# Transposes of the first part as pairs of 64-row halves, norms ahead as listed steps, and new written orders for the first part and the transition

## The chip, the cores and the metric

The kernel runs on one core of a Trainium2 chip. The metric is the device time of one execution in microseconds (us); the median of three runs before the change is 1122.0 us. The engines are TensorE (PE for matmuls, PEld for its weight loads), VectorE (DVE), ScalarE (ACT), GpSimd (POOL) and SyncE (SP), whose queue issues nearly all DMAs. Matmul results go to PSUM, eight banks of 512 float32 columns on 128 partitions.

## The reference

Two blocks follow each other. The first is attention with random features, for 8 batches, 8 heads, 576 rows and 64 columns a head, and 128 features; the second mixes by Fourier transforms and applies a two-layer perceptron, 512 wide and 2048 hidden.

```python
def phi(x):                                   # x is q or k, scaled; omega is 128 x 64
    h = np.einsum('bhsd,md->bhsm', x, omega) - np.sum(x * x, axis=-1, keepdims=True) / 2.0
    h = h - np.max(h, axis=-1, keepdims=True)
    return np.exp(h) / np.sqrt(m)
kv = np.einsum('bhsm,bhsd->bhmd', k_p, v)
z = np.sum(k_p, axis=2)
out = np.einsum('bhsm,bhmd->bhsd', q_p, kv) / (np.einsum('bhsm,bhm->bhs', q_p, z)[..., None] + 1e-06)
# the heads side by side: x is (8, 576, 512)
u = x + np.real(np.fft.fft(np.fft.fft(x, axis=1), axis=2))
un = (u - mean(u)) / np.sqrt(var(u) + 1e-06)
result = u + np.maximum(un @ w_ch1, 0.0) @ w_ch2
```

All is float32 in the kernel. The two weight matrices arrive as float64 and are narrowed on the chip.

## The kernel before

**First part.** A pair of heads is one unit of the attention, n = 0 to 31 (B * NP), three units in flight (`attn`, L668). `loads` brings k and q of a unit into one tile kq of 18 x 64 columns (L471, L474) on SP's queue. `transposed` (L590) turns the nine 128 x 128 pieces of kq on PE against the 128 x 128 identity `ident` (L607), in groups of 4, 4 and 1, each group into one bank; `evicted` (L611) copies a bank to the tile kqT, on ACT or DVE (L621, L623), and the bank is free. Matmuls with omega (L701) follow, for the first six units as 64-row halves of the array, later as 64 x 64 quarters. DVE takes the maxima (L644), ACT the exponentials e (L661). L735 makes kv in quarters. The nine pieces of e that belong to q are turned in the same way into qeT (groups of 1, 4, 4), but here the eviction also reorders rows, so that mirrored rows stand where the Fourier part wants them: each group is copied in two pieces, one of them read backwards. L782 and L790 multiply qeT with kv, two 64-column halves at a time; the quotient goes to x.

Once per batch `mix` (L823) folds x on DVE and POOL and multiplies with cosine and sine tables (L894, L904, L944, L955). `residual` (L980) joins the cosine part and the sine part: ACT copies one bank to bmp (L988), DVE makes difference and sum in three pieces each (L993 twice, L996), and both are added to x on DVE or POOL (L1005, L1006). The sum u goes to DRAM (`us`).

Beside it, `narrow` (L522) makes float32 weights out of the float64 ones in five elementwise steps, over ACT, POOL and DVE (L534 or L532, L537 to L544, L550). `plain_of` (L1205) runs the perceptron of the first four tiles of 128 tokens in the ordinary way (L1236, L1259): PE work that can stand wherever the attention leaves room. `norm_of` (L1130) normalises a tile and turns it with four 128 x 128 transposes (L1172, evicted at L1176). `warm` (L574) issues six matmuls on zeros at the start, `first` (L581) turns omega (L586).

**Second part.** Eight blocks of 512 tokens are multiplied by two levels of a seven-product scheme (L1727, L1878 and, for the second layer, L2178), from w1, its sums and sums stored in DRAM. The normalised tokens of later blocks reach it turned, through DRAM tiles `turned`. For blocks 1 to 3 (j) this is done by `ahead` (L1573): twelve tiles are loaded, normalised and turned in 32 x 32 pieces on DVE, nine of them in buffers that the attention leaves (kq, kqT), three in late ones. `wash` (L2288) marks three banks with matmuls on the identity before the second part (L2298).

**The order.** The kernel's Python code runs a listing: streams of `Step`s with an engine, buffers to take and give and banks ("bank" is one, "duo" two neighbouring ones). The next step is not chosen by cost; it is read from strings, `PICKS` (which waiting step is next, and for a step with a choice which engine) and `BANKS` for the first part, `PICKS2` and `BANKS2` for the second. So each engine's order is written out, and an instruction that waits holds all behind it on its engine. The pieces of `ahead` stand outside the listing: `BETWEEN` and `BETWEEN2` say after which number of placed steps a generator is advanced.

Of the kernel before, what the change touches and what calls it, by code (L numbers as in the profile page):

```python
# [41 lines left out]
class Clock(NamedTuple):  # L42
# [25 lines left out]
PICKS = (  # L68
    "40e0fff03eafdaege3OcdceefdcOdeccfgda37ghj0gjj7hlP79aj7ik97i8S7efhjffeHldffiehdjfdOihgihidaKedbhhciff"
    "ecgOfeejdfdPdeeedgifdffdefd8aiii88jhd8jP8b99i8e8jcddghjgheiifcOcdciieicgPgdefJcdghbkededfgcRbggb79ij"  # L70
    "8hi7hjafN9Haj9gfffeg8eif8hcej1jccc7ehidbhffLigebfbe6766gggfcbjahj9Ofghhjj8dQkkgT6jghff8de6dUjfhbgegh"
    "cefhafjUf8jgciSjOckkhjakkaeikggjlioklnhSgodoXON7l7l6nnj9icadc97cibf98ejH88a7edhMlhkmjjaQVijihkkfplSm"
    "okliljjilVaghVhnmljkmpjkhhnmkimlgglmbjpjjQ9d9alafhhdjlaMdjback0j766k7lh4g896ck6gkki77gij5ijhgj6dimni"
    "3ndjgi6Kc4jldlKikbkaijLhf75dcjlmklk36ci45jciekajkkkk5kihokeaeoLaioNlencidonbSiljjcmjjkboijTUUhgcfkik"
    "hiflkmeFF99nol5m8jT7naabda89Rbj97ecdl8cjilOgifkQb4acahg57ebbgabgdjkdTkk6eceebb5f9dg4R6ce486ggg6egfhh"
    "fg4g9egf5cbdhgPRhhcgjhggejigibLmHnbedijj6NOb7biihi9bgihMkaffPa8cijdhbdghbaeibNefffacjicigifi99975ih5"
    "jgj8699ajfg6g7fgefd65bO6Kalkkgd5jgjikagfldliPJpeoaeeefgdejadgilgScljiii5e65k56kl57k7j67S9lilk9gliih6"
    "ffkgec4fg4dbgg7fedaiP5gfbheefilddddddeghg9kbfncgghcfkkafkagGngb65p5Hopoj4bhoanbelli68bjjl5b7dlhighhi"
    "lflhpkgiWomjknmmmkimnjbjhn9jkmFKkfFgedccff6Wf7idUVhi8Th3fogbqp8fgmkeSdjna7ckenoghmnmffnjeo79q6547oa4"
    "nlkpd7aceonnc8blSVicilbhmjim8fh7SnnIl5mUkfjgfhhfhihg8ghfbS4kjf83j4lllb79jei8mnkblfnmmiolpilOUi9Mh5l5"  # L80
    "pmnaem79jjVmkbblek5iji9a9kffTgjikhiShfgjafhgfigh4g50PPP0ba5Pdh9dghdK77hgfdcbg8OO988jMehefibjjkellfcc"
    "PcdhQMihfQcffbKCf82b3c98cbcdcd6a299efgddbJaGQQbefLa9ecf74gg986HRgf9idg8kQeheff7be6ff2e5cc8fbcgdKP8f8"
    "9hN9Lc999bddcHcNb7Oc9effegd7ibhQeQ8haf7ccghhlUikhHW5lWmm5dkMQGM71fS6d1gdb99747ifddhIfdhhdhfdbihgiljn"
    "gWgijgg93ekKl8kEhIIbT3jjKgkb9k9eTfhkhlje34m49974iG66h68faHe6e7a79982975aI94a39c8cM8b4aa7ab984fge8eLM"
    "98b86ce8PbFPc9cbe6cKPf3a9b94fIdIQeJKbd876eJPdc5fNb7ffbf9JSS8RiLa4a7gPbajfgg8gdfhg2i2787Hf6OcdIN5d3LH"
    "accd46ddeKK72dJc7bbaa4bb9a9bc7c0777dghhdf7Bfddebd76ff1fddIe9949438686bc6aca85348dHcG7a5be957b55d1544"
    "9Gc1F5a9a68446344584584E59189970955888574443113301110"
)

BANKS = (  # L90
    "0102346120164024306243643016204164024320632462014021604606245062345042604670426420340267407231640260"
    "4524016460620240674206206415704602546064320143607264506402346234062732017426042106147026740260462462"
    "0410652604632452017205467402624060404256174302642060245016745202642016420634520520650162505605260250"
    "1675602501605204672016204567627450264102316742067460260462045642062637230724672402630145420640106240"
    "5264023026731602454230412046450416725730620424670121726154305610207453"
)

PLACES = "kkktttkktuuu"  # L100


BETWEEN = (
# [3 lines left out]
)  # L107


BETWEEN2 = (  # L110
    "006390119901259015590198902149023690236a0262a0265a0301a0329a0355a0426a0486b0528b0528b0550b0552b0563b"
    "0578b"
)
# [262 lines left out]
def kernel(  # L376
# [21 lines left out]
    KD = DM // 2 + 1  # L398
    QD = DM // 4
    KE = QD + 1  # L400
    K0 = DM // 8 + 1
    CV = 512
    P = 128

# [1990 lines left out]
```

## Time and profile before

| | us |
|---|---|
| median of three runs (1120.99 to 1122.96) | 1122.0 |
| profiled execution, first to last instruction (its span; no other time of it is given) | 1119.2 |
| first part, up to the first L1727 | 417.8 |
| second part | 701.4 |

In the profile, the first table gives the busy time of each engine. The windows give it stage by stage. In a group of instructions "L607 PE MATMUL banks<-ident,kq 128\*128 128x128" line 607 multiplies, with 128 rows and 128 columns of weights, a streamed operand (ident) into banks; 64\*128 are 64 rows and 128 columns. A float32 matmul that is no transpose appears as two passes, so as two records; a transpose is one. A record's own duration (some 275 ns for 128 columns) is longer than the distance between two of them, since they overlap; what one costs is read from a run of them on the chain or from two starts on the timeline.

### The profile page before, as it was taken

How to read it: one execution, taken by the hardware profiler on the slowest of the kernel's cores; microseconds unless marked ns; L12 is line 12 of the kernel's file. 1: busy time of each engine (PE TensorE's matmuls, PEld its weight loads, DVE VectorE, ACT ScalarE, POOL GpSimd, SP SyncE). 2: the span in 40 equal slices, each digit the busy share in tenths (PEclk: the TensorE clock that was granted, in tenths of full speed). 3: DMA queues.
4: the chain of work that ended last, by engine and by line, in shares of the span. 5: the costliest groups of instructions: out<-in, count | busy, mean ns of one | idle time of the engine just before them, and what ended most of it. 6: DMA issues, size and time to landing. Idle time of an engine off the chain costs nothing.

```text
span 1119.2 us, 31666 instructions
## 1 busy us (share of the span) xinstructions
PE 1108.4 (99%) x12467; PEld 1000.4 (89%) x12467; DVE 888.7 (79%) x1685; ACT 539.5 (48%) x1644; POOL 390.6 (35%) x401
## 2 busy tenths in 40 slices
PE   9999999999999999999999999999999999999998
PEld 7888888879868778999999889999889999889998
DVE  6999999987576767687697777888677888568895
ACT  7998898856536455623214452223463223331221
POOL 2443443553563348634413464000365000152000
PEclk9999999999999999999999999999999999999999
DMA  8856766665674669798896778747678656546453
GB/s 243 243 174 188 242 180 191 183 208 176 216 232 156 194 172 343 224 314 262 260 326 224 226 216 248 207 148 238 206 207 261 207 155 216 170 152 220 146 160 105
DMA packets 196549, 236.13 MB, mean 211 GB/s; under 512 B 53808, under 2 KB 120624, under 8 KB 196400
## 3 DMA queue, kind: packets, MB, share of 16 engines
q1 hardware_dynamic: 195904, 233.83, 68.1%
q8 instruction: 99, 1.62, 0.6%
q14 instruction: 50, 0.41, 0.1%
q10 hardware_dynamic: 496, 0.26, 0.1%
HBM read 182.13 MB, written 56.10 MB: 213 GB/s over the span
## 4 chain that ended last, share of the span: by engine, by line
PE 92%; DVE 3%; ACT 2%; DMA 2%; issue 0%; POOL 0%; SPq 0%; DVEq 0%; ACTq 0%
PE banks L2178 31%; PE banks L1727 27%; PE banks L1236 5%; PE banks L701 5%; PE banks L607 5%; PE banks L1259 5%; PE banks L1878 4%; PE banks L735 3%; PE banks L782 2%; PE banks L944 2%; PE banks L894 1%; ACT e L661 1%; DVE nmx L644 1%; PE banks L904 1%; DMA unw<-turned 1%; DMA raw<-in_moe_w_ch_dram 1%
## 5 line engine op out<-in xcount | busy, mean ns | idle before, releaser
L2178 PE MATMUL banks<-wl,sums 128*128 128x128 f32 x1792 | 219.8, 275 | 0.0
L2178 PEld LDWEIGHTS banks<-wl,sums 128*128 128x128 f32 x1792 | 210.6, 192 | 1.0 <-issue 0.3
L661 ACT ACTIVATE e<-banks,nmx 128x128 f32<-128x128 f32 x576 | 165.7, 441 | 23.3 <-DVE nmx L644 22.9
L644 DVE TENSOR_REDUCE nmx<-banks 128x8 f32<-128x1024 f32 (+1 forms) x96 | 89.3, 951 | 16.8 <-PE banks L701 12.4
L2178 PE MATMUL banks<-wl,hid 128*128 128x128 f32 x768 | 99.2, 275 | 0.3 <-DVE part L2154 0.3
L2178 PEld LDWEIGHTS banks<-wl,hid 128*128 128x128 f32 x768 | 92.8, 192 | 1.2 <-DVE part L2154 0.8
L2149 ACT ACTIVATE s<-banks 128x128 f32<-128x128 f32 x112 | 30.9, 277 | 113.6 <-PE banks L2178 103.5
L1727 PE MATMUL banks<-unw,wxw 128*128 128x256 f32 x352 | 85.4, 379 | 0.0
L701 PE MATMUL banks<-om,kqT 64*64 64x128 f32 (+1 forms) x2088 | 79.0, 275 | 1.7 <-ACT kv L751 1.3
L701 PEld LDWEIGHTS banks<-om,kqT 64*64 64x64 f32 (+1 forms) x2088 | 64.5, 138 | 12.7 <-issue 3.2
L2178 PE MATMUL banks<-wl,hx 128*128 128x128 f32 x576 | 74.2, 275 | 0.4 <-DVE part L2154 0.4
L1727 PEld LDWEIGHTS banks<-unw,wxw 128*128 128x128 f32 x352 | 66.6, 190 | 8.9
L1727 PE MATMUL banks<-rx,wxw 128*128 128x256 f32 x288 | 70.8, 379 | 0.0
L2178 PEld LDWEIGHTS banks<-wl,hx 128*128 128x128 f32 x576 | 69.4, 192 | 0.8 <-DVE part L2154 0.6
L1752 ACT ACTIVATE s<-banks 128x512 f32<-128x512 f32 x65 | 38.5, 596 | 65.1 <-PE banks L1727 60.0
L1727 PE MATMUL banks<-ttw,wxw 128*128 128x256 f32 x288 | 69.8, 379 | 0.0
L1236 PE MATMUL banks<-unT,w 128*128 128x128 f32 x512 | 65.4, 279 | 1.7 <-DVE qeT L621 1.7
L550 POOL TENSOR_TENSOR w<-w,raw 128x512 f32<-128x512 f32 x28 | 37.6, 1351 | 77.3 <-DVE raw L544 68.1
L2227 POOL TENSOR_TENSOR more<-more,part 128x512 f32<-128x512 f32 x2 | 2.6, 1315 | 176.6 <-ACT part L2220 176.6
L1236 PEld LDWEIGHTS banks<-unT,w 128*128 128x128 f32 x512 | 60.2, 192 | 4.5 <-issue 2.3
L1727 PEld LDWEIGHTS banks<-rx,wxw 128*128 128x128 f32 x288 | 54.5, 190 | 7.3
L1727 PEld LDWEIGHTS banks<-ttw,wxw 128*128 128x128 f32 x288 | 54.5, 190 | 7.3
(287 smaller groups left out, 2442.3 us busy)
## 6 DMA issues: line engine op xcount, KB each, us to landing
wl<-w2l SPq DMA_DIRECT2D x245, 256.0 KB, 3.9
wxw<-w1x SPq DMA_DIRECT2D x120, 256.0 KB, 3.1
raw<-in_moe_w_ch_dram SPq DMA_DIRECT2D x32, 512.0 KB, 4.8
kq<-in_k_dram SPq DMA_DIRECT2D x32, 288.0 KB, 4.5
kq<-in_q_dram SPq DMA_DIRECT2D x32, 288.0 KB, 4.5
vd<-in_v_dram SPq DMA_DIRECT2D x32, 288.0 KB, 5.4
ur<-us SPq DMA_DIRECT2D x30, 256.0 KB, 5.2
w2l<-sums SPq DMA_DIRECT2D x14, 512.0 KB, 4.9
```

The costliest lines, as they stand in the source:

```text
L550: eng.tensor_tensor(out=dst, in0=dst, in1=lof, op=ALU.add)
L607: nc.tensor.transpose(ps[:, (j - j0) * 128 : (j - j0 + 1) * 128], src(j), ident[:])
L644: nc.vector.tensor_reduce(nmx[:, :, 0:num], pps[:, :, 0 : MF * num].rearrange("p b (c m) -> p b c m", m=MF), axis=AX.X, op=ALU.max, negate ...
L661: nc.scalar.activation(out=e[:, c + (i if num == 1 else 0), :], in_=pps[:, i, MF * c : MF * c + MF], func=AF.Exp, bias=nmx[:, i, c : c + 1],)
L701: nc.tensor.matmul(pps[cols, c, MF * m : MF * m + MF], lhsT=kqT[rows, j, cols], rhs=om2[rows, :],)
L735: nc.tensor.matmul(kvp[cols, i, 0 : D + 1], lhsT=feature(r)[rows, cols], rhs=vds[n % NV][rows, r, :], start=(r == 0), stop=(r == R - 1),)
L1236: nc.tensor.matmul(hp[:, 0:TP], lhsT=w1[:, dc, 128 * fc : 128 * fc + 128], rhs=unTs[key][:, dc, :], start=(dc == 0), stop=(dc == NDC - 1),)
L1259: nc.tensor.matmul(yp[:, 0:DM], lhsT=hs[fc][:, 128 * i : 128 * i + 128], rhs=w2[:, fc, :], start=(fc == 0), stop=(fc == NFC - 1),)
L1727: nc.tensor.matmul(ps[:, span * f : span * f + span].rearrange("f (b q) -> f b q", q=Q), lhsT=left[:, P * f : P * f + P], rhs=right, start ...
L1752: nc.scalar.activation(out=s[:], in_=ps, func=AF.Copy)
L1878: nc.tensor.matmul(cell.rearrange("f t (b q) -> f t b q", q=Q), lhsT=w[:, d, col : col + 128], rhs=right[:, :, d].rearrange("f (t b) q -> ...
L2178: nc.tensor.matmul(ps[:, 0:128], lhsT=left[:, f], rhs=wls[head(j), i, n][:, f], start=start and f == 0, stop=(f == 3), skip_group_check=True,)
```

## The change

- **Halves.** Each 128 x 128 transpose becomes two instructions on 64 rows of the source and a 64 x 64 block of `ident`; the halves write to two neighbouring banks, r = 0 and 1 (`half_turned`). The groups are 4 and 5 for kqT and 5 and 4 for qeT, each in a "duo"; there is one copy per group. `ident` gets permuted blocks off its diagonal, so that the mirrored order of qeT is made by the transpose itself, which writes every fourth column of its bank (`spaced`); the second factor's columns are addressed accordingly in L782 and L790. Omega's and the norms' transposes are halved too.
- **Identity.** `ident` comes by DMA, first on SP's queue, instead of from POOL.
- **Mixing.** L944 writes even columns of the spectrum to every second column of the bank and odd ones between; the tables are ordered to suit. For two of the three row groups `residual` uses five ACT instructions, then two DVE additions of 257 columns instead of six pieces; the third group has the pieces as before.
- **Narrowing.** The third step may run on POOL, as two instructions.
- **Norms ahead** are ordinary steps of the listing: nine in the first part (buffers kq and turned), three in the second.
- **Orders.** All `PICKS` and `BANKS` strings are new.
- `NTURN` is 32, the number of units; what is for n >= NTURN never runs (a transpose of whole units on DVE, with loads in blocks).

```diff
+    eyes = np.zeros((2, D, 2, D), np.float32)
+    h_, s_, t_ = np.meshgrid(np.arange(2), np.arange(2), np.arange(16), indexing="ij")
+    turn_ = (32 * h_ + 2 * np.where(s_ == 1, 15 - t_, t_) + s_).ravel()
+    for r in range(2):
+        eyes[r, np.arange(D), r, np.arange(D)] = 1.0
+        eyes[r, turn_, 1 - r, np.arange(D)] = 1.0
+    nc.sync.dma_start(ident[:], nc.inline_tensor(eyes.reshape(128, 128), name="k_eyes").ap())
...
-    make_identity(nc, ident[:])
...
+    def half_turned(to, src, turn=False):
+        for r in range(2):
+            rows, cols = slice(D * r, D * r + D), slice(D * (r ^ turn), D * (r ^ turn) + D)
+            nc.tensor.transpose(to(r), src[rows], ident[rows, cols])
+
+    def spaced(ps, r, at, c):
+        out = ps[:, r, :]
+        return bass.AP(out.tensor, out.offset + at + c, [list(out.ap[0]), [128, 2], [67 - 2 * c, 2], [4, 16]])
...
             yield Step(
                 PE,
-                0.109 * m,
+                0.062 * m,
+                mode="rows",
                 after=after(j0, j1),
-                take=("bank",) + (("turned",) if j0 == 0 else ()),
+                take=("duo",) + (("turned",) if j0 == 0 else ()),
...
-                nc.tensor.transpose(ps[:, (j - j0) * 128 : (j - j0 + 1) * 128], src(j), ident[:])
-            yield Fork(evicted(dst, b, j0, j1, makes, order))
+                i = j - j0
+                def to(r):
+                    if not mirror:
+                        return ps[:, r, D * i : D * i + D]
+                    if j == 0:
+                        return ps[:, r, 0:D].rearrange("q (s t) -> q t s", s=2)
+                    c = (j - 1) % 4
+                    return spaced(ps, r, D * (j - c - j0), c)
+                half_turned(to, src(j), mirror and j > 0)
+            yield Fork(evicted(dst, b, j0, j1, makes, mirror))
...
-            ((0, 4), (4, 8), (8, R)),
+                ((0, 4), (4, R)),
...
-            ((0, 1), (1, 5), (5, R)),
+            ((0, 5), (5, R)),
...
-                    ab[p1 * n : p1 * n + np_, n, cols],
+                    ab[p1 * n : p1 * n + np_, n, m:KD:2],
...
-        yield Step(ACT, 0.28, take=("bmp",), give=(b1,))
...
+        if c < NL:
+            yield Step(ACT, 0.62, take=("bmp",), bias=0.1)
+            bmp, (aa, mi, pl) = taken()
+            nc.scalar.activation(out=mi[:, KD:], in_=pb[:, KD : KD + 1], func=AF.Copy)
+            nc.scalar.activation(out=pl[:, KD:], in_=pb[:, KD : KD + 1], func=AF.Copy, scale=-1.0)
+            nc.scalar.activation(out=aa[:, 1:KD:2], in_=pa[:, 1:KD:2], func=AF.Copy)
+            for k, mid in ((0, mi), (2, pl)):
+                nc.scalar.activation(out=aa[:, k:KD:4], in_=pa[:, k:KD:4], func=AF.Identity, bias=mid[:, KD:])
+            for last, (dst, op) in enumerate(((mi, ALU.subtract), (pl, ALU.add))):
+                yield Step(DVE, 0.34, give=(b0, b1) if last else (), bias=-0.1)
+                nc.vector.tensor_tensor(out=dst[:, 0:KD], in0=aa[:, 0:KD], in1=pb[:, 0:KD], op=op)
...
-        yield Step(DVE, 0.61, give=("sign",), port=True, bias=-0.99)
...
+        step = Step({DVE: 0.61, POOL: 3.0}, give=("sign",), port=True, bias=-0.99)
+        yield step
+        if step.eng == POOL:
+            nc.gpsimd.tensor_scalar(lof, lo, 2.0**-52, None, op0=ALU.mult)
+            nc.gpsimd.tensor_tensor(out=lof, in0=lof, in1=sign[:].bitcast(F32), op=ALU.mult)
...
-        yield Step(PE, 0.437, take=("bank",), give=("u",))
+        yield Step(PE, 0.26, mode="rows", take=("duo",), give=("u",))
...
+            half_turned(lambda r: tp[:, r, D * dc : D * dc + D], u[:, 128 * dc : 128 * dc + 128])
...
-        yield Step(NONE, give=(b,))
+        yield Step(NONE, after=("held",), give=(b,))
```

More of the change, by code (lines that the diff above doesn't have):

```diff
@@ L411 @@
     NWIDE = 6
+    NTURN = 32
     TP = 128
@@ L726, in attn @@
             mode="quarters",
-            after=tuple(("e", n, t) for t in range(3)) + (("vd", n),),
+            after=tuple(("e", n, t) for t in ((0, 1, 2) if n < NTURN else (0, 2, 3))) + (("vd", n),),
             take=("duo",),
@@ L1065 @@
     unTs = {}
-    Q = 32
     turned = {}
@@ L2359 @@
     listing.run(
-        [wash(), late_turns(), late_norms(), halves(), load_leaves(), token_sums(0), w1_sums(), w1_inner(), w1_stored()],
+        [wash(), late_turns(), late_norms(), halves(), load_leaves(), token_sums(0), w1_sums(), w1_inner(), w1_stored()]
+        + [ahead(3, i, "ur", late) for i in range(1, TB // 128)],
         picked(PICKS2, 3),
         BANKS2,
-        betweens(BETWEEN2),
     )
```

456 lines of the change are left out of this document (282 added, 174 removed).

## The prediction

> **What bounds the kernel now.** First the page's busy shares and its chain of waits, which ask for the engine that sets the end; then the windows, stage by stage, since a share of the whole span is a mean over two very different stages; then the timeline, for where the first stage ends.
>
> ```profile
> PE 1108.4 (99%) x12467; PEld 1000.4 (89%) x12467; DVE 888.7 (79%) x1685; ACT 539.5 (48%) x1644; POOL 390.6 (35%) x401
> ...
> PE 92%; DVE 3%; ACT 2%; DMA 2%; issue 0%; POOL 0%; SPq 0%; DVEq 0%; ACTq 0%
> ```
>
> ```profile
> 0.00:100.00 100.00, 95.51 (x2003) 80.26 (x2004) 87.97 (x177) 88.64 (x323) 36.00 (x41) 1.00 0.75 217
> 100.00:200.00 100.00, 99.72 (x2212) 88.73 (x2211) 94.44 (x221) 85.65 (x306) 46.54 (x44) 1.00 0.67 201
> 200.00:300.00 100.00, 100.00 (x1954) 84.04 (x1953) 79.84 (x164) 70.65 (x252) 49.04 (x52) 1.00 0.60 183
> 300.00:419.00 119.00, 117.29 (x1362) 88.33 (x1361) 84.64 (x204) 55.49 (x176) 54.41 (x71) 1.00 0.62 198
> 419.00:1119.00 700.00, 695.86 (x4945) 659.00 (x4944) 541.80 (x921) 239.07 (x593) 204.64 (x194) 1.00 0.71 218
> ```
>
> ```profile
> 417.81 1.06 PE L1727 MATMUL banks<-unT,w 128*128 128x128 f32 x8
> ```
>
> The columns of the windows are PE, weight loads, DVE, ACT, POOL, granted clock, DMA share, GB/s. PE is busy in 412.5 of the first 419 us and in 695.9 of the last 700, at full clock, and the chain of waits is 92% PE: work taken from PE shortens the kernel, as long as the others keep up. DVE (94 of 100 us between 100 and 200) and ACT (89 of the first 100) are the next. The first part ends where L1727 starts, at 417.8 us; all transposes lie before it.
>
> **The transposes.** 576 at L607, 32 at L1172 and one at L586 become 1218 halves: 64 rows of weights, 64 columns streamed, two at a time in separate row halves of the array.
>
> ```profile
> 0.00:419.00 419.00, 82.96 (x576) 63.96 (x576) 1.00 0.66 200
> ...
> L1172 PE MATMUL banks<-ident,u 128*128 128x128 f32 x32 | 4.9, 282 | 0.0
> ```
>
> ```profile
> 310.49 1.97 PE banks L607 x18
> ```
>
> ```profile
> 7.31 1.16 PE L701 MATMUL banks<-om,kqT 64*128 64x128 f32 x16
> ...
> 368.44 1.15 PE L782 MATMUL banks<-kv,qeT 128*64 128x65 f32 x32
> ...
> 369.42 0.40 PE L790 MATMUL banks<-kv,qeT 128*64 128x65 f32 x8
> ```
>
> ```profile
> 26.40 1.21 PE banks L735 x72
> ```
>
> L607's window row (82.96 us for 576) holds waits; a whole transpose costs 1.97/18 = 0.109 us where nothing waits. No transpose by halves is in the trace, so its pair is bounded by neighbours that stream as little. L782 runs two 65-column passes at once: 32 passes between 368.44 and 369.42, 0.061 a pair. L735 runs four: 1.21/72 x 4 = 0.067. Row halves do run together: L701 here issues 16 passes of 128 columns, two at a time, in 1.16 us, of which the last 0.28 is its own length: 0.88/8 = 0.11 a pair, what one alone costs. The lower end is 0.055 (half of 0.109), the upper 0.109 (no gain). I take 0.062, by L782, which streams as much: 609 x 0.047 = 28.6 us less; the ends are 32.9 and 0.
>
> The halves need another tile shape than whole matmuls. A change of shape is seen here:
>
> ```profile
> 12.19 0.66 PE L607 MATMUL banks<-ident,kq 128*128 128x128 f32 x4
> ...
> 12.78 0.49 PE L701 MATMUL banks<-om,kqT 64*128 64x128 f32 x4
> ```
>
> The last L607 starts 0.28 before 12.85, at 12.57; L701 follows 0.21 later instead of 0.11, so a change costs about 0.09. The listed orders of both kernels hold 224 changes of shape ahead of the second stage before, 252 after: +2.5 us.
>
> **Evictions and residual.** Two evictions of 512 and 640 columns take the place of three (kqT) and five (qeT, in pieces); each group now holds two banks, not one.
>
> ```profile
> L623 ACT ACTIVATE qeT<-banks 128x256 f32<-128x256 f32 x104 | 34.4, 444 | 4.1 <-PE banks L607 2.4 <-issue 1.2
> L623 ACT ACTIVATE kqT<-banks 128x512 f32<-128x512 f32 x49 | 29.3, 635 | 17.5 <-PE banks L607 17.2
> L623 ACT ACTIVATE qeT<-banks 128x64 f32<-128x64 f32 x48 | 10.0, 304 | 3.7 <-PE banks L607 3.7
> L623 ACT ACTIVATE kqT<-banks 128x128 f32<-128x128 f32 x20 | 6.3, 320 | 1.1 <-PE banks L607 0.9
> L988 ACT ACTIVATE bmp<-banks 128x258 f32<-128x258 f32 x16 | 6.2, 387 | 7.2 <-PE banks L955 6.8
> L1145 ACT ACTIVATION_READ_ACCUMULATOR junk<-u 128x1 f32 x16 | 3.1, 192 | 0.0
> ```
>
> ```profile
> 0.00:419.00 419.00, 25.12 (x67) 1.00 0.66 200
> ```
>
> ```profile
> L544 DVE SCALAR_TENSOR_TENSOR raw<-raw,sign 128x512 f32<-128x512 uint32 x32 | 22.0, 687 | 0.6
> L993 DVE SCALAR_TENSOR_TENSOR bmp<-banks,bmp 128x65 f32<-128x65 f32 x32 | 10.5, 329 | 4.2 <-ACT bmp L988 4.2
> L993 DVE SCALAR_TENSOR_TENSOR bmp<-banks,bmp 128x64 f32<-128x64 f32 x32 | 10.5, 327 | 0.0
> L621 DVE COPY kqT<-banks 128x512 f32<-128x512 f32 x15 | 10.2, 683 | 0.9 <-PE banks L607 0.8
> L996 DVE TENSOR_TENSOR bmp<-banks,bmp 128x128 f32<-128x128 f32 x32 | 9.0, 280 | 0.0
> L854 DVE TENSOR_TENSOR half<-half 128x257 f32<-128x257 f32 x14 | 5.9, 423 | 0.2
> L532 POOL TENSOR_SCALAR w<-raw 128x512 f32<-128x512 f32 x8 | 12.9, 1618 | 19.7 <-DMA raw<-in_moe_w_ch_dram 19.7
> ```
>
> By the new listing ACT evicts 44 of 512 columns (0.60 each, 29.3/49) and 40 of 640 (0.75): 56 us where the four rows sum to 80, -24. DVE's are 20 of 0.68 and 24 of 0.85: 34 us instead of 25 (L621's window row), +9. In the residual 16 ACT copies of 0.39 become 16 times five small ones (2 of 0.19, 3 of about 0.30): +14; DVE drops 30.0 us (L993, L996) for 32 additions of 257 at 0.42 = 13.4: -17. Five of the 0.69 us steps of L544 and twelve of L534 go to POOL, at 1.62 for each pass and two passes for L544's: POOL +35, idle for more than half of every window. Net ACT about -10, DVE about -11: against a first part 5% shorter both keep the share of time that they had. So these edits are costed at nothing of their own; PE covers them. What is bought with that cover is that PE, issuing faster into banks taken two at a time, waits more often for an eviction. PE idles 6.5 us of the first 419 by the windows; I add 3, between -4 (fewer, larger groups wait less) and +15 (the whole loss of cover between 100 and 200, where DVE has 5.6 us left in 100, repeated over the part).
>
> **The start.** The identity is no longer made on POOL but loaded on SP's queue ahead of the first k and q, and the warm-up matmuls of L578 stand behind the first qeT.
>
> ```profile
> 0.72 0.40 SPq L471 DMA_DIRECT2D kq<-in_k_dram  x1
> ...
> 1.04 2.93 PE L578 MATMUL banks<-ur 128*128 128x128 f32 x12 [1.04 <-DVE ur L492]
> ...
> 1.18 0.42 SPq L474 DMA_DIRECT2D kq<-in_q_dram  x1
> ...
> 3.84 0.81 PE L607 MATMUL banks<-ident,kq 128*128 128x128 f32 x4
> ```
>
> An issue takes 0.46 of the queue, so every load behind it and the first transpose (3.84) come 0.5 later: +0.5, on the path. The 12 passes leave a stretch in which PE had nothing to do for one in which it may: 12 x 0.109 = +1.3, 0 if PE waits there anyway. They ran at 2.93/12 = 0.24 each, twice the later 0.109; now the first transposes meet that state: 0 to +2.5, and +0.5 taken, since DVE and ACT set the pace there.
>
> **Norms ahead, orders.** The nine norms run ahead in the same kq and turned buffers and with nearly the same instructions as before, only listed as steps; three follow in the transition. At the seam the last norm's transposes stand six L1259 matmuls ahead of L1727 instead of sixteen, while DVE has four stream transposes and the sums tt between. L1727 queues all PE work behind it; if tt is late, PE waits: 0 to +3, I take 0.5. The listed PE order of the two kernels is the same again from about the 540th matmul of the second part on.
>
> Sum: -28.6 + 2.5 + 0.5 + 1.3 + 0.5 + 3 + 0.5 = -20.3, from the profiled span of 1119.2 to 1098.9. The runs' median, 1122.0, lies 2.8 above that span: 1101.7.
>
> **Rivals.** *Strided writes.* The mirrored qeT halves now write every fourth column of a bank, and L944 every second one.
>
> ```profile
> 0.00:419.00 419.00, 22.77 (x192) 18.96 (x192) 1.00 0.66 200
> ```
>
> No matmul of before writes with a step. If a stepped write took twice its time, 256 pairs add 256 x 0.062 = 15.9 and L944's row up to 22.8: -20.3 + 38.7 gives 1140, and the kernel is slower from a toll of half that. Against it: the old qeT evictions read with a step and reversed, at 34.4/104 = 0.33 for 256 columns, beside 0.60 for 512 straight ones: the banks charge nothing for steps there. [...] No run yet shows a matmul of that kind; I give it 0.07.
>
> *Loads in turn.* Each half still loads 128 columns of weights.
>
> ```profile
> L2178 PEld LDWEIGHTS banks<-wl,sums 128*128 128x128 f32 x1792 | 210.6, 192 | 1.0 <-issue 0.3
> L607 PEld LDWEIGHTS banks<-ident,kq 128*128 128x128 f32 x288 | 32.2, 141 | 7.5 <-issue 2.7 <-ACT e L661 1.8 <-DMA kq<-in_q_dram 0.4
> L701 PEld LDWEIGHTS banks<-om,kqT 64*128 64x128 f32 x216 | 13.7, 187 | 2.6 <-issue 1.0 <-ACT kv L751 0.6 <-ACT kqT L623 0.2
> L735 PEld LDWEIGHTS banks<-vd,e 64*64 64x64 f32 x2304 | 38.0, 134 | 4.5 <-issue 1.3 <-ACT kqT L623 1.0 <-ACT w L534 0.6
> ```
>
> Half the rows do not shorten a load (187 beside 192), half the columns do (134). If a pair's loads set 0.109, nothing is saved and the sum is +8.3 with the waits, about +5 without: 1127, slower. Against it: a transpose's own load (141) is as short as one of 64 columns, and those sustain 0.061 a pair at L782. 0.08. [...]
>
> *DVE sets the pace.* If the first part shrinks only by what DVE loses, 11 us, and the start's 2.3 stay, the result is 1113. For it stand DVE's 94 of 100; against it its 80 in 200 to 300. 0.13.
>
> *Both better ends at once*: pairs at 0.055 (-4.3) and waits of -4 in place of +3: 1101.7 - 11.3 = 1090. 0.06. *That halves do not run side by side* is the loads' rival at its end; DVE's own transposes (NTURN) never run, as n stays below 32.
>
> **How the numbers follow.** The forecast has 0.66 and its own range 1095 to 1109: waits of -4 to +10 at 0.062 a pair; 0.055 and 0.067 alone give 1097 and 1105. 0.2% (2.2 us) is what a measurement of this kernel can tell from none. Faster: 0.66 + 0.13 + 0.06 = 0.85; slower: 0.07 + 0.08 less 0.03 for tolls that just cancel: 0.12; same 0.03. The range 1093 to 1117 takes in DVE's case and part of the better one, and leaves out the two slower ones.
>
> **What would show it.** Right: pairs of halves about 0.06 apart, their row near 37 us for 609 instead of 88; L1727's successor starting near 398; L944's passes still 0.11 apart; DVE and ACT shares as before. Wrong: halves at 0.1 a pair, stepped rows slower than kqT's straight ones, or PE below 96% in the first 400 us.

## The result, and the profile after

The changed kernel takes 1156.7 us (median of four runs, 1152.1 to 1159.5) beside 1122.5 for the kernel before on the same chip: a ratio of 1.0296, 95% interval 1.0268 to 1.0324. The forecast was 1101.7. The profiled execution took 1152.1, its span is 1150.3, 31 above the span before; it is the shortest of the four, 4.6 below their median.

The page of the changed kernel, its busy shares and its chain of waits:

```profile
PE 1105.7 (96%) x13076; PEld 993.2 (86%) x13076; DVE 892.6 (78%) x1602; ACT 527.1 (46%) x1578; POOL 411.1 (36%) x424
...
PE 73%; DVE 12%; DMA 5%; ACT 4%; issue 3%; SPq 1%; POOL 1%; DVEq 0%; ACTq 0%; POOLq 0%
```

Its windows (columns as before), and from its timeline the start of the second part:

```profile
0.00:100.00 100.00, 85.70 (x2086) 73.96 (x2086) 81.34 (x148) 78.88 (x266) 56.01 (x53) 0.98 0.71 203
100.00:200.00 100.00, 93.18 (x2274) 80.75 (x2277) 93.02 (x177) 76.94 (x269) 58.15 (x60) 1.00 0.66 195
200.00:300.00 100.00, 98.24 (x2223) 80.54 (x2216) 85.45 (x158) 69.41 (x242) 39.62 (x43) 1.00 0.50 144
300.00:430.00 130.00, 126.61 (x1558) 94.39 (x1557) 85.47 (x185) 63.09 (x211) 58.07 (x75) 0.97 0.70 220
430.00:1150.00 720.00, 702.00 (x4952) 663.60 (x4950) 547.33 (x938) 238.80 (x594) 199.27 (x195) 1.00 0.69 213
```

```profile
429.79 1.06 PE L1875 MATMUL banks<-unT,w 128*128 128x128 f32 x8
```

PE is no longer the bound that it was: 73% of the chain, not 92%. The loss lies in two places. The first part ends at 429.8 instead of 417.8. PE's busy time there fell by 8.8 us (412.5 to 403.7), its idle time grew by 19.8 (6.5 of 419 to 26.3 of 430). The second part, whose matmuls are the same, takes 720.5 instead of 701.4; PE idles 18.0 us of it, before 4.1.

The transposes themselves came out nearly as priced. Groups of the changed kernel, then of the kernel before, in the first part:

```profile
L715 PE MATMUL banks<-ident,kq 64*128 64x64 f32 x576 | 30.8, 237 | 9.2 <-DMA kq<-in_k_dram 4.5 <-DMA kq<-in_q_dram 1.0 <-ACT e L797 0.9
L715 PE MATMUL banks<-ident,e 64*128 64x64 f32 x576 | 28.4, 229 | 0.7 <-DVE kv L899 0.2 <-ACT e L797 0.2 <-DVE qeT L769 0.2
```

```profile
L607 PE MATMUL banks<-ident,e 128*128 128x128 f32 x288 | 43.7, 280 | 0.9 <-ACT e L661 0.9
L607 PE MATMUL banks<-ident,kq 128*128 128x128 f32 x288 | 42.0, 279 | 0.4 <-ACT e L661 0.2
```

From every second start of the 1218 halves to the next one of its row half it is 62 ns (median): a pair costs 0.062 us, for kq, written in straight columns, as for e, written with a step. The first pair of an uninterrupted row takes longer, 112 ns. The busy time of the rows fell from 85.7 to 59.2; it stays far above 576 times 0.062, since a record (230 ns) is longer than that distance and the ends of a group count whole. Of the idle time ahead of the kq halves 5.5 us are the first loads, which the warm-up used to fill.

What TensorE waited for in the first part, longest first (in all, times, longest), in the changed kernel and then in the kernel before:

```profile
PE banks L885 <- issue: 4.8, 4, 2.8
PE banks L715 <- DMA kq<-in_k_dram: 4.5, 1, 4.5
PE banks L932 <- issue: 2.2, 2, 1.7
PE banks L848 <- issue: 1.5, 1, 1.5
PE banks L885 <- DMA vd<-in_v_dram: 1.4, 1, 1.4
PE banks L715 <- ACT e L797: 1.1, 3, 0.8
```

```profile
PE banks L1236 <- DVE qeT L621: 1.7, 1, 1.7
PE banks L701 <- ACT kv L751: 1.3, 3, 0.7
PE banks L607 <- ACT e L661: 1.1, 4, 0.4
PE banks L578 <- DVE ur L492: 1.0, 1, 1.0
```

All idle time of the first part, added up by what ended it: for results of VectorE and ScalarE, evictions among them, 8.4 us beside 5.5 before; for loads 6.9 beside none; "issue" 9.3 beside 0.4; gaps under 0.15 us 1.8 beside 0.6.

Three of the first six are "issue": TensorE stood still and waited for no semaphore. The longest stands at 311 us; the windows around it:

```profile
310.00:312.00 2.00, 1.24 (x78) 1.10 (x70) 1.59 (x2) 0.69 (x4) 1.92 (x3) 1.00 1.12 345
312.00:314.00 2.00, 0.00 (x0) 0.00 (x0) 0.00 (x0) 0.00 (x0) 2.00 (x2) 0.86 0.20 38
314.00:316.00 2.00, 1.99 (x20) 1.51 (x22) 0.00 (x0) 1.31 (x5) 2.00 (x3) 0.50 0.04 9
316.00:318.00 2.00, 2.00 (x21) 1.88 (x22) 1.29 (x3) 0.97 (x3) 2.00 (x4) 0.50 1.04 279
```

It stops amid the 72 matmuls of a kv step, VectorE and ScalarE run dry behind it, and for 6.8 us afterwards the granted clock is 0.50. Counting TensorE's instructions from the start shows what the place is: all eight such pauses of 0.6 to 3.1 us (11.1 us together, from the start of one instruction to the start of the next) stand at place 193 or 194 of a block of 256 instructions, and end 1.3 to 1.5 us after the next 16 KB packet of the instruction queue has landed.

```
starts  pause  line   place of 256   after landing
 34.0   1.95   L932   194            1.40
 56.1   1.85   L848   194            1.47
 90.4   0.62   L715   193            1.42
123.2   1.42   L885   193            1.44
133.4   0.65   L885   193            1.31
138.3   0.78   L932   193            1.36
311.0   3.05   L885   193            1.50
366.6   0.81   L885   193            1.32
```

The kernel before has two of 0.4 to 0.5 us at such places. The halves bring 609 more matmuls with a weight load each, and let TensorE pass its instructions faster (a pair of halves is four in 62 ns, a whole transpose two in 109).

In the second part it waits for other things; its waits there, and SyncE's queue from the timeline:

```profile
PE banks L2326 <- DMA wl<-w2l: 3.2, 2, 1.7
PE banks L1875 <- DVE hid L1918: 2.9, 1, 2.9
PE banks L1875 <- ACT s L1900: 2.9, 1, 2.9
PE banks L1875 <- DVE tt L1517: 2.0, 1, 2.0
```

```profile
518.46 5.55 SPq L2222 DMA_DIRECT2D wl<-w2l  x8
532.72 0.52 SPq L1759 DMA_DIRECT2D turned<-ur  x1
533.33 1.57 SPq L2222 DMA_DIRECT2D wl<-w2l  x3
```

SyncE issues nothing from 524.0 to 532.7: it waits with the store of a norm ahead (L1759) for VectorE's transpose (L1757, 531.99 on VectorE's timeline), and the next twenty entries behind it are loads, three of wl and seventeen of wx. TensorE's 2.9 us for L1918 at 530 lie behind the same transpose on VectorE; the two waits for wl follow between 579 and 599.

### The profile page after: what moved, and what is told of

It reads as the page before. It is cut to its first block, busy times and chain, and to the rows that moved or that the text cites. A ratio compares the mean times of both kernels' runs of the same rounds, so it can differ in the third digit from the quotient of the medians.

```text
span 1150.3 us, 32716 instructions
## 1 busy us (share of the span) xinstructions
PE 1105.7 (96%) x13076; PEld 993.2 (86%) x13076; DVE 892.6 (78%) x1602; ACT 527.1 (46%) x1578; POOL 411.1 (36%) x424
## 3 DMA queue, kind: packets, MB, share of 16 engines
q8 instruction: 103, 1.69, 0.6%
## 4 chain that ended last, share of the span: by engine, by line
PE 73%; DVE 12%; DMA 5%; ACT 4%; issue 3%; SPq 1%; POOL 1%; DVEq 0%; ACTq 0%; POOLq 0%
PE banks L2326 28%; PE banks L1875 24%; PE banks L848 4%; PE banks L1395 3%; PE banks L2026 3%; ACT e L797 2%; DVE nmx L780 2%; PE banks L932 2%; PE banks L715 2%; PE banks L1418 2%; PE banks L885 1%; DMA wl<-w2l 1%; PE banks L1094 1%; DVE w L655 1%; DMA unw<-turned 1%
## 5 line engine op out<-in xcount | busy, mean ns | idle before, releaser
L797 ACT ACTIVATE e<-banks,nmx 128x128 f32<-128x128 f32 x576 | 158.1, 413 | 34.8 <-DVE nmx L780 34.6
L780 DVE TENSOR_REDUCE nmx<-banks 128x8 f32<-128x1024 f32 (+1 forms) x96 | 89.1, 952 | 19.1 <-PE banks L848 15.0
L848 PE MATMUL banks<-om,kqT 64*64 64x128 f32 (+1 forms) x2088 | 85.4, 279 | 3.0 <-issue 1.5
L1875 PE MATMUL banks<-unw,wxw 128*128 128x256 f32 x352 | 85.4, 379 | 0.0
L848 PEld LDWEIGHTS banks<-om,kqT 64*64 64x64 f32 (+1 forms) x2088 | 68.6, 141 | 12.2 <-issue 2.6
L1875 PEld LDWEIGHTS banks<-unw,wxw 128*128 128x128 f32 x352 | 66.6, 190 | 8.9
L1900 ACT ACTIVATE s<-banks 128x512 f32<-128x512 f32 x65 | 38.4, 596 | 73.7 <-PE banks L1875 55.5
L1875 PE MATMUL banks<-ttw,wxw 128*128 128x256 f32 x288 | 70.0, 380 | 0.9 <-ACT banks L1907 0.9
L1875 PE MATMUL banks<-rx,wxw 128*128 128x256 f32 x288 | 70.8, 379 | 0.0
L1831 POOL TENSOR_TENSOR hid<-hid 128x512 f32<-128x512 f32 x35 | 47.7, 1376 | 40.1 <-DVE hid L1831 7.2
L1875 PEld LDWEIGHTS banks<-ttw,wxw 128*128 128x128 f32 x288 | 54.3, 190 | 8.8 <-ACT banks L1907 1.7
L1875 PEld LDWEIGHTS banks<-rx,wxw 128*128 128x128 f32 x288 | 54.5, 190 | 7.3
```

The lines of the kernel that those rows point to most:

```text
L780: nc.vector.tensor_reduce(nmx[:, :, 0:num], pps[:, :, 0 : MF * num].rearrange("p b (c m) -> p b c m", m=MF), axis=AX.X, op=ALU.max, negate ...
L797: nc.scalar.activation(out=e[:, c + (i if num == 1 else 0), :], in_=pps[:, i, MF * c : MF * c + MF], func=AF.Exp, bias=nmx[:, i, c : c + 1],)
L848: nc.tensor.matmul(pps[cols, c, MF * m : MF * m + MF], lhsT=kqT[rows, j, cols], rhs=om2[rows, :],)
L1831: eng.tensor_tensor(out=o, in0=l, in1=r, op=op)
L1875: nc.tensor.matmul(ps[:, span * f : span * f + span].rearrange("f (b q) -> f b q", q=Q), lhsT=left[:, P * f : P * f + P], rhs=right, start ...
L1900: nc.scalar.activation(out=s[:], in_=ps, func=AF.Copy)
```

## The experiments

Ratios are to the kernel before in the same series, medians, with 95% intervals; the end of the first part is the first L1875 (or its line) of the profiled execution.

### Halves and banks in the old order

**e1, the halves alone.**

```diff
-                take=("bank",) + (("turned",) if j0 == 0 else ()),
+                take=("duo",) + (("turned",) if j0 == 0 else ()),
...
-                nc.tensor.transpose(ps[:, (j - j0) * 128 : (j - j0 + 1) * 128], src(j), ident[:])
+                half_turned(to, src(j), mirror and j > 0)
```

> The kernel before with the halved transposes alone: two neighbouring banks, the permuted identity by DMA, one copy per group, groups of 4, 4, 1 and 1, 4, 4 as before, and before's written-out orders of both parts (26 of the 498 PE steps had to move by up to three places, for banks). Theory 'orders' (the halves do save PE work; the loss of 34 us comes with the new orders): 1122.5 - 28.6 + 5 for more changes of tile shape and the identity, about 1099, PE idle as before. Theory 'halves' (a faster PE runs into waits for the other engines and for its own instructions in whatever order): 1110 to 1130, with PE's idle time in the first part grown by 12 us or more and its idle places spread over all units.

1190.1 us, 1.058 (1.054 to 1.063); the first part ends at 485.6, the second takes 701.7 as before. "Halves" was nearer, but far short. Without the new orders the change is worse. **e5** turns whole pieces in the same places and the same two banks.

```diff
-                half_turned(to, src(j), mirror and j > 0)
+                nc.tensor.transpose(ps[:, i // 2, 128 * (i % 2) : 128 * (i % 2) + 128], src(j), ident[:])
```

> The first experiment's kernel, its orders and its banks unchanged, but the nine pieces of kq and e are turned whole again, two to each of the two banks (groups of one in one bank); left out is the mirrored order of the rows of qeT. Theory 'banks' (two banks a group, 871 banks taken in the first part where the kernel before takes 670, make PE wait for evictions): still 1170 to 1200, the halves themselves gaining or losing less than 15. Rival 'halves' (the small matmuls themselves bring the stalls): back to 1120 to 1135.

1181.0, 1.052 (1.050 to 1.054). Its groups in the first part:

```profile
L671 PE MATMUL banks<-ident,e 128*128 128x128 f32 x288 | 48.0, 285 | 8.3 <-ACT e L720 2.5 <-ACT qeT L694 2.4 <-DVE qeT L692 1.2
L671 PE MATMUL banks<-ident,kq 128*128 128x128 f32 x288 | 45.3, 284 | 10.8 <-DVE kqT L692 3.8 <-ACT kqT L694 3.5 <-ACT y L976 2.0
```

The same whole transposes that waited 0.4 and 0.9 us in the kernel before wait 10.8 and 8.3. Transposes of kq need nothing that VectorE or ScalarE make; what they wait for is a bank that an eviction still holds. Evictions ended 25.8 of the 46.7 us that PE idles in the first part of e5, and 2.0 of 6.5 in the kernel before. Two banks a group cost 58 us in this order, with nearly every transpose at its old price; e5 also keeps e1's loaded identity, its single copy a group and its halved norms, and none of these was undone alone. On top of it the halves lose another 9 instead of gaining 26. The granted clock goes with that: 34.1 us of e1's first part ran at half clock after pauses, 13.7 of e5's. The order of e1 and e5 had needed a new deal of the banks; **e15** is the control for that, with one bank a group.

```diff
-        picked(PICKS, 1),
+        picked(PICKS, 3),
```

> A control for the experiments in the old order: the kernel before, computing the same in the same way with one bank a group, but with the first part's banks dealt anew by the rule that those experiments used (239 of 470 choices differ, 18 listing steps moved by a few places). Theory 'two banks' (the 58 us of the fifth experiment are the second bank's): 1122 to 1128. Rival (the new deal and the moved steps cost it): 1150 or more, and the experiments in the old order say little about two banks.

1123.4, 1.001 (1.000 to 1.002): the deal costs nothing here. **e6** asks whether halves pay where the listing has a bank to spare.

```diff
+                mode="rows" if (n, name, j0) in HALVED else "whole",
+                take=("duo" if (n, name, j0) in HALVED else "bank",) + (("turned",) if j0 == 0 else ()),
```

> The kernel before with 34 of its 64 groups of four of kq turned as halves into two banks, those for which the listing of before has a bank to spare (no more than eight taken at any step); the order of before, 16 listing steps moved. By PE's work: 34 x 4 x 0.047 = 6.4 us less, 27 more changes of tile shape x 0.09 = 2.5 more: 1119. Theory 'banks': banks spare in the listing are what lets TensorE run ahead; 3 to 15 us more, 1126 to 1138.

1131.3, 1.007 (1.006 to 1.008), 12 above PE's sum and within "banks". A spare bank in the listing was not spare in time: evictions end 6.1 us of PE's idle time here, 2.0 before. Not all of the 12 is theirs: in this profile the full clock comes at 10.6 us, before at 4.2.

### Whole transposes in the new order

**e2.**

```diff
+                if i < 4:
+                    nc.tensor.transpose(ps[:, i // 2, 128 * (i % 2) : 128 * (i % 2) + 128], src(j), ident[:])
+                    continue
```

> The changed kernel with its new orders, but eight of nine transposes of kq and e in whole 128x128 pieces again (the ninth of a group of five stays halved); left out is the mirrored order of the rows, so the values of the first part are others. 512 pairs go from 0.062 back to 0.109 us, 24 us of PE work. Theory 'orders' (fixed waits of the order, which a busier PE does not shorten): 1175 to 1182. Theory 'halves' (PE is ahead of what feeds it and waits): the work goes into the idle time, 1157 to 1168, with fewer idle places on PE.

1161.9, 1.034 (1.032 to 1.037): 39 us above the kernel before, with eight of nine transposes of kq and e whole, so that the loss does not hang on the halves. It is 5 us above the changed kernel, at the edge of the noise: the runs overlap (1157.7 to 1164.0 beside 1152.1 to 1159.5). Its window of the first part:

```profile
0.00:438.00 438.00, 425.43 (x7610) 342.76 (x7611) 344.39 (x663) 289.38 (x984) 208.63 (x230) 1.00 0.62 188
```

PE is busy 21.7 us more than in the changed kernel (425.4 beside 403.7) and idle 13.7 us less (12.6 beside 26.3); the pauses at block edges fall from eight to three. So in the new order the halves buy time, 8 us of the first part by these two profiles (5 by the medians), and two thirds of what they save turns into waiting: of the 13.7 us, 4.9 at "issue", 6.1 for results of VectorE and ScalarE, 1.8 for loads, the rest in short gaps. Some of the 21.7 is not the price of a transpose: counted in the traces, e2 changes the tile shape 367 times in the first part, the changed kernel 283 times, the kernel before 257. **e7** frees one bank of each group of four of e2.

```diff
+                if m == 4:
+                    nc.tensor.transpose(ps[:, 0, 128 * i : 128 * i + 128], src(j), ident[:])
+                    continue
```

> The second experiment's kernel (whole transposes in the new order), with the groups of four written to one bank of their two and copied from there, so that nothing waits for the other bank; order and bookkeeping are unchanged, the mirrored order of the rows stays left out. Theory 'banks': 5 us or more below the second experiment's 1161.9. Rival (the new order's waits are not for banks): within 3 us of it.

1161.6: no difference. In the new order, made for two banks, the second bank of these groups is not what TensorE waits for. What e5 showed of banks holds for the old order.

### The mixing alone

**e9.**

```diff
-                    ab[p1 * n : p1 * n + np_, n, cols],
+                    ab[p1 * n : p1 * n + np_, n, m:KD:2],
```

> The kernel before with the changed mixing alone: L944 writes every second column, five ACT copies and two DVE additions in two of three row groups; the order of before, 24 listing steps moved for banks. My forecast: nothing of its own, 1121 to 1125. Rival 'strided writes' (a stepped write costs twice): 1133 to 1140. Rival 'banks' (both banks of the mixing held until the second addition instead of one given back after the copy): 1126 to 1135, without slower L944 rows.

1127.6, 1.0036 (1.0021 to 1.0051). The stepped writes are not slower, by this kernel's group:

```profile
L981 PE MATMUL banks<-sd_sb,y 128*128 128x129 f32 (+3 forms) x96 | 15.6, 285 | 0.3 <-ACT qeT L660 0.3
```

15.6 us, as L944's 96 matmuls on sd_sb took before. The 4 us fit the rival "banks", at its low end; that they are the bank's was not shown apart.

### TensorE's instruction blocks

**e11, shifted blocks.**

```diff
+        for _ in range(32):
+            nc.tensor.matmul(ps[:, 0:16], lhsT=ur1[:, 0:128], rhs=ur1[:, 0:16])
```

> The fourth experiment's kernel (warm-up first) with 32 more matmuls of 16 columns on zeros behind the six, 64 passes and so 128 more instructions at the front of TensorE's queue. Theory 'instruction supply' (TensorE starves at every 256th instruction where it has used up 256 faster than the next block comes): the long pauses without a wait leave the instructions where they stood (L932 near 34 us, L848 near 56) and stand at other instructions, again at places 193 or 194 of 256, counted with the 128. Rival (something at those instructions stops TensorE that the records do not show): they stay at the same instructions. The time: within 6 us of 1151.7 by both, plus up to 2 for the 64 passes.

The six pauses (10.7 us) stand at other instructions, at place 193 or 194 with the 128 counted in: in kv, nd and omega steps at 45.0, 56.2, 60.6, 97.8, 148.1 and 284.7. These pauses belong to the block's edge. The time, 1163.4, missed the forecast by 4: the 64 small passes took 10.5 us of TensorE (3.8 to 14.3), not 2, and 10.2 us ran at half clock at the start. **e13** adds traffic.

```diff
+        extra = dram.tile([P, R, D], F32, name=f"extra{n}")
+        nc.sync.dma_start(extra[:], v[b, 2 * pr : 2 * pr + 2].rearrange("i (p r) d -> (i p) r d", r=R))
```

> The changed kernel with one more copy on SyncE's queue behind each load of v: 288 KB from v to an unused place in DRAM, 32 of them, a third more traffic in the first 300 us. Theory 'supply held up by data' (the 256-instruction blocks come late because they share the DMA engines with the loads): TensorE's pauses without a wait at the block edges grow from 11.5 us to 16 or more, in number and in length, and the first part by 8 or more. Rival (a block takes the same time whatever else moves): the pauses stay at 9 to 13 us.

Eleven pauses, 13.0 us instead of 11.1, and the time is the same (1156.4). The rival holds, at its upper end: that a block comes later when more moves is not shown. e3, below, has the changed kernel's first part without the added copies; of pauses over 0.5 us it has nine, 12.0 us together, and e13 nine with 11.8.

### The second part and the start

**e3, the old order of the second part.**

```diff
-    "0240000260200190270270230240280170220240170260230260230250270260270280230230230230230240230310310270"
...
```

> The changed kernel, its first part untouched, but the second part's steps in the order of the kernel before; the three norms ahead that belong there stand where the pieces stood before. Theory 'second order' (SyncE's and VectorE's places of the norms ahead hold up the loads and the banks behind them): the second part takes 701 to 706 us instead of 720, the whole about 1138 to 1142. Rival (the second part is late because the first leaves its last rows late, whatever the order): no more than 5 us gained, 1152 to 1157.

1142.5, 1.018 (1.015 to 1.021), 14 below the changed kernel, the only edit that gained this much; between the two profiled spans it is 9. The store of the last norm ahead stands further back in SyncE's queue here, straight behind its transpose (540.82 to 541.51 on VectorE):

```profile
536.96 3.00 SPq L2212 DMA_DIRECT2D wx<-w1x  x4
540.01 0.42 SPq L2177 DMA_DIRECT2D w1x<-so  x1
541.54 0.52 SPq L1759 DMA_DIRECT2D turned<-ur  x1
542.32 0.46 SPq L2212 DMA_DIRECT2D wx<-w1x  x1
```

SyncE stands still for 1.1 us ahead of it, not 8.7, and neither a wait for wl nor the one for L1918 is left. (Ahead of an earlier norm's store, at 476.11, it stands still for 7.1 us here too, and no wait of TensorE follows: this held queue cost nothing.) The second part still takes 712.4, and not 701 to 706; 6.5 us of that are TensorE's waits in the first 11 us, for the first sums of tokens (tt) and the first evictions behind them, and 3.4 are lost to the half clock that follows.

**e4 and e17, the warm-up first**, e17 with the old order of the second part.

```diff
-    "0010160060160150000170160000040160010080100110100160150150160150160170110140141140131160140151170160"
+    "0150160010150060150140000160150000040150010080100090100150140140150140150160100130131130121150130141"
```

> The changed kernel with the six warm-up matmuls moved back to the front of TensorE's queue, nothing else moved. Theory: full clock from about 4.2 us on instead of 9.6, and the 1.4 us of the six under the wait for the first load: 3 to 4 us less, 1153. Rival (what comes later waits for loads anyway): within 1 us of 1156.7.

> The third and fourth experiments together: the changed kernel with the warm-up first and the old order of the second part. If the two are separate costs they add: 1156.7 - 14.2 - 5.0 = 1137 to 1139, and the first part still ends 8 us or more later than in the kernel before. Rival (the start's gain is lost again in the first part's waits): 1141 to 1144. Neither theory puts it below the kernel before.

> The twelfth experiment again (warm-up first, old order of the second part) with the banks of the changed kernel kept. Theory 'dealt banks': the two costs add after all, 1136 to 1140, and the first part ends by 427. Rival (the start's gain is lost in later waits): 1142 to 1146, as e12.

e4 took 1151.7, 5 below the changed kernel. e12, with both edits, 1144.2, above e3's 1142.5. Both had their first part's banks dealt anew; with the banks of the changed kernel e17 took 1141.9, still e3's time. In e17's profile TensorE has its full clock from 3.9 us on, and nothing of that reaches the end. In those of e4 and e12 it comes at 10.1, no earlier than in the changed kernel (9.6): the warm-up at the front does not by itself bring the clock. In the traces with the warm-up in front it came between 3.9 and 6.0 in seven and between 10.1 and 10.6 in three, with the warm-up behind between 8.3 and 10.6. So e4's 5 us are not shown to be the clock's; its profiled span, 1152.3, is no shorter than the changed kernel's.

**e8, e18, e10, e16, e14: the seam**, all on e3's kernel.

```diff
-    "0130120191120120121160170080170081130130140141080170140010080160160040001150090090170041121171170131"
+    "0130121120180120121160170080170081130130140141080170140010080160160040001150090090170041121171170131"
```

> The third experiment's kernel (changed kernel, old order of the second part), with all steps of the last batch's mixing moved 45 places forward in the listing, so that 3 plain 1.72 us steps and 14 of 0.89 stand behind its first matmuls and not before them. Theory 'cover' (the new order leaves 7.6 us between the last mixing matmul and the seam, the old one 17, and the second part starts before its rows are there): the second part takes 702 to 706 instead of 712 us, the whole 1132 to 1136. Rival (the seam's gaps come from the nine norms ahead, whatever the mixing does): no change, 1140 to 1144.

> The eighth experiment again (old order of the second part, last batch's mixing 45 places earlier), with the banks of the changed kernel kept for every step. Theory 'cover' (the rows of the last batch come too late for the second part; mixing them earlier mends that): the first part ends at 427 to 433 and the second takes 703 to 708, 1131 to 1138 in all. Rival (the chain from the last attention unit to the rows is long in itself, so that TensorE waits before the seam for what it waited for behind it): 1141 to 1149.

> The third experiment's kernel with nine of the weight sums (L1643) that stand in VectorE's queue between 380 and 396 us put on GpSimd, orders unchanged. Theory 'VectorE at the tail' (24.1 us busy of 25 between 375 and 400; what the seam waits for is late there): 9 x 0.68 = 6 us earlier for the last mixing and norms, the second part 704 to 708 us instead of 712, the whole 1134 to 1138. Rival (GpSimd takes 1.3 us for each, the sums are one chain, and their stores and loads come late in turn): 1142 or more.

> The tenth experiment again, with the banks of the changed kernel kept. In e4, e8, e10, e12 and e14 the first part's banks had been dealt anew by the rule of the control e15, which cost the old order 0.1%; in the new order it was not checked. This kernel differs from e10 by the banks alone and from e3 by nine sums alone. Theory 'dealt banks' (in the new order the deal costs the 12 us by which those first parts are longer): the first part ends at 427 to 431 us, and the whole is 1134 to 1142. Rival (the moved sums lengthen the first part): 1148 to 1153, as e10.

> The third experiment's kernel with the w2 sums (44 steps, between 311 and 395 us there, in the kernel before between 247 and 368) moved forward in the listing so that they begin where the weights are narrowed, at 257, and end near 350; nothing else moves. Theory 'late filler on VectorE' (15 us of sums stand ahead of the last folds and make the last mixing, its rows and the seam late): the second part takes 702 to 706 us and the first is not longer, 1130 to 1136 in all. Rival (the chain from the last attention unit to the second part is long anyway, or TensorE waits for VectorE earlier instead): 1140 to 1148.

None gained: 1149.5, 1157.8, 1151.5, 1149.9 and 1165.9 us. In e8 and e10 the second part came down to 706 and 705 us, as forecast, and the first grew to 441. But that is the new deal of banks and not the moved work: e12, with banks dealt by the same rule and neither the mixing nor the sums moved, has 440.7 and 705.5. TensorE's longest wait near the seam, the same in e10 and in e12, is now one ahead of it, at the matmuls of the wash:

```profile
PE banks L2446 <- DVE ur L1431: 6.4, 1, 6.4
```

With the banks kept, the second part is 711.7 in e16 and 710.9 in e18, as in e3 (712.4), and the first ends at 435.6 and 444.6 instead of 429.0. TensorE's waits in e18 from 300 us on:

```profile
PE banks L1044 <- DVE ur L1431: 5.8, 1, 5.8
PE banks L715 <- DVE u L1332: 4.2, 1, 4.2
PE banks L1875 <- ACT s L1900: 4.0, 1, 4.0
```

Ten microseconds of waiting for VectorE are new ahead of the seam, and the wait behind it (L1900, 4.3 in e3) is still there. In e14 TensorE waited 7.3 us for a load of k that stands behind stores of the earlier sums on SyncE's queue. No order tried here gets the last rows to the second part sooner; which work would have to go is open.

## Why the prediction was wrong

- **The price of a pair: right.** 0.062 us within a row. *Loads in turn* is wrong, since pairs do follow each other at 62 ns and not at 109. *Strided writes* is wrong too: stepped and straight halves keep the same distance (62 ns), L1094's passes are 112 ns apart as L944's were, and e9's row is unchanged (15.6 us).
- **The step that failed: the terms for TensorE's waiting, "I add 3" and, at the seam, "I take 0.5".** PE's idle time grew by 19.8 us in the first part, above the upper end of 15, and the seam cost 19.1. The 3 were to cover waits for evictions and were sized by VectorE's spare time. Waits for results of VectorE and ScalarE did grow by about that, 2.9. What grew were waits that this term did not think of: "issue", nearly all of it at the edges of instruction blocks, by 8.9, for which the sum has nothing, and loads by 6.9, most of them the first loads, for which it has 0.5.
- **The work fell by less than summed.** PE was to be busy 24.3 us less in the first part; it was 8.8 less. Give each moment of its busy time to the matmul that started last: the transposes then take 55.7 us instead of 77.5, 21.8 less, where 28.6 less 2.5 for the tile shapes makes 26.1; all other matmuls, the same as before, take 14.0 more. 5.1 us are the clock, which falls to half for 3.4 or 6.8 us after the longer pauses (10.2 us of the first part), a term that the sum lacks; the first 9.6 us at half clock, before 4.2, add to it (L848's records last 418 ns there, as in the half clock from 36.9 to 40.4, and 272 at full clock). The rest is spread over all lines, and its cause is open; waits shorter than a record (220 to 280 ns) would look like this.
- **Banks and orders.** That each group holds two banks was noted and given no price of its own. In the old order two banks a group cost 58 us (e5). The new order wins much of that back: with whole transposes the first part ends at 438.2 instead of 477.1. But that is still 20 us longer than before; by e7 it is not the second bank of the groups of four, and an estimate puts 10 of it on 110 more changes of tile shape at the 0.09 us of the prediction. The second part takes 724.0 there. For the new orders the sum has 0.5, and 2.5 for tile shapes; with whole transposes the whole costs 39 (e2).
- **The seam.** I had noted four stream transposes and tt on VectorE there, and that the PE order was the old one from about the 540th matmul on; what I left out was the queue of SyncE. Eight of the 19.1 are the second part's order (e3); that within it the places of the norms ahead did it is read from the traces, where TensorE's 2.9 us for L1918 and 3.2 for wl are gone. Of the other 11, e3 shows 6.5 as waits for the first sums and evictions and 3.4 as half clock; what makes the last rows late is open.
- **The start: +2.3.** e4 gave back 5.0, e17 beside e3 0.6. As a term of a sum it is not defined: the clock came early or late with the same warm-up in front (at 3.9 us in e17, at 10.1 in e4 and e12).
- **Mixing and evictions at nothing:** the mixing cost 4 (e9), in the old order. The evictions alone were not tried.
- ***DVE sets the pace*** gave 1113. VectorE's busy time in the first part fell by 1.6 us (346.9 to 345.3) and not by 11, and its share did not rise; the waits for it that count stand at the seam.

## What to carry to other kernels

A cheaper matmul that needed a second bank was paid for with run-ahead, in an order made for one bank (58 us in e5): price the bank first, by giving the old matmul two banks and changing nothing else. A term for waits has to name each supplier, for one may stay as forecast (results of VectorE and ScalarE, 2.9 us more) while another grows ("issue", 8.9 more, and loads, 6.9). Where an engine at 99% is made faster, its gain is worth only what its suppliers have to spare, and the instruction stream was one of them here (eight pauses, 11.1 us). When a step is moved into a listed order, look at the in-order queue that issues its store: what is due behind that store waits for the step (SyncE issued nothing for 8.7 us, with twenty loads behind).

## What the runs showed of the hardware

In the changed kernel TensorE stood still at the edges of its instruction blocks: eight pauses in the first part, 11.1 us together, all at place 193 or 194 of 256. e11 moved the instructions by 128, and its six pauses (10.7 us) stayed at these places. In the changed kernel's profile 103 packets of 16 KB (1.69 MB) came on the instruction queue for some 26,500 instructions, one for 256. In the first part the packet of a block starts to load a median of 1.2 us after TensorE has entered the block before, at most 2.3 us ahead of that, and takes 1.0 us: the loads run about one block ahead here. That was not enough where small matmuls follow each other at some 15 ns an instruction (a pair of halves is four instructions in 62 ns): pauses of 0.6 to 3.6 us, in the changed kernel and in e1, e2, e3, e4, e6 and e11.

In the changed kernel's trace the pause of 1.95 us at 34.0 is followed by a granted clock of 0.50 from 36.9 to 40.4, the one of 1.85 at 56.1 by none. In the traces of the changed kernel and the kernel before, all ten changes of the granted clock lie whole multiples of 3.4133 us after the first full clock, within 1 ns (8, 9, 89, 91 and so on; 326 in the kernel before). Cut into such windows, the two traces show 655 at full clock. Six are followed by half clock: PE idled 1.81, 1.82, 1.97, 2.18, 2.32 and, at the end of the changed kernel, 3.41 us of them. The others are followed by full clock: PE idled at most 1.71 us of any. The pause at 34.0 lies within one window (33.5 to 36.9, 1.81 us idle), the one at 56.1 is split at 57.4 (1.14 us idle in the one window, 1.17 in the next). So in five of the six PE worked for 1.1 to 1.6 us of the window, and half clock followed all the same. The slow stretches of the changed kernel's trace, but for the one that its end cuts off, are 3.4 us long and once 6.8.
